# Gated attention and a SiLU layer on one core: the state's product with values as the stationary operand, and four weight loads issued earlier

## The chip, the core and the metric

The kernel runs on one core of a Trainium2 chip. A core has a matrix engine (TensorE), a vector engine (VectorE), a scalar engine for activation functions (ScalarE), a general engine (GpSimd) and a queue engine (SyncE, "SP" in the profile), each with its own instruction stream. They share an on-chip memory of 128 partitions (SBUF) and a small accumulator memory (PSUM) that TensorE writes. Transfers between DRAM and SBUF, or inside SBUF, are issued from SP, ScalarE or GpSimd and carried out by the DMA engines.

The metric is the device time of one execution in microseconds (us). The kernel before takes 665.35 us (median of 3 runs, 663.98 to 667.26).

## What is computed

Two blocks follow each other. The first is a gated linear recurrence with a complex decay per channel; B = 4 batches, H = 8 heads, S = 768 positions, D = 48 channels per head. The second is a feed-forward layer with SiLU, 384 to 2048 to 384, over all 3072 tokens.

```python
def _attn_ref(q, k, v, a_re, a_im):
    B, H, S, D = q.shape
    mag = np.sqrt(a_re * a_re + a_im * a_im)
    scale = np.minimum(mag, 0.999) / (mag + 1e-06)
    a_re_n, a_im_n = (a_re * scale, a_im * scale)
    # S_re, S_im: (B, H, D, D), zero at the start
    for t in range(S):
        ar, ai = (a_re_n[:, :, t, :, None], a_im_n[:, :, t, :, None])
        new_re = ar * S_re - ai * S_im
        new_im = ar * S_im + ai * S_re
        kv = np.einsum('bhd,bhe->bhde', k[:, :, t], v[:, :, t])
        S_re, S_im = (new_re + kv, new_im)
        y[:, :, t] = np.einsum('bhd,bhde->bhe', q[:, :, t], S_re)
    return y

def _moe_ref(x, w_in, w_out):
    h = x @ w_in
    g = h * (1.0 / (1.0 + np.exp(-h)))
    return g @ w_out
```

The kernel does not step through the positions. It cuts them into chunks of 128 and multiplies keys and queries with the running decay (magnitude and angle), so that a chunk's output is a masked product of queries and keys with the values, plus a product of the queries with the state that earlier chunks left. A complex channel becomes two real ones, so keys and queries have 2 x 48 = 96 channels per head.

## The kernel before

There are 24 chunks (4 batches of 6), taken two at a time: step p handles chunks 2p (called A) and 2p + 1 (called B). Chunk n + 4 continues chunk n of the same batch. While a step's attention runs, TensorE also works through the feed-forward layer of the pair before.

The state that chunk n hands on is one product per head, with the rotated keys `kr` (128 positions x 96 channels) as the stationary operand and the values (128 x 48) moving. VectorE adds the old state and multiplies by the chunk's decay:

```python
def state(n):
    x = X[n]
    if place(n)[1] == NCH - 1:                   # the last chunk of a batch hands nothing on
        return
    ps = p_m.tile([D2, H, D], F32, tag="m", name=f"s{n}")          # D2 = 96
    for h in range(H):
        nc.tensor.matmul(ps[:, h], lhsT=x["kr"][:, h].rearrange("p c d -> p (c d)"),
                         rhs=x["v"][:, h], start=True, stop=True)
    x["s"] = ps
    if n >= STRAIGHT:                            # STRAIGHT = 4
        carried_on(n)

def carried_on(n):
    x = X[n]
    ps = x["s"]
    new = att.tile([D2, H, D], F32, tag="S", name=f"S{n + B}", bufs=5)
    by = decs[:, n].unsqueeze(2).to_broadcast([D2, H, D])
    if "S" in x:
        nc.vector.tensor_tensor(out=new, in0=ps, in1=x["S"], op=ALU.add)
        nc.vector.tensor_tensor(out=new, in0=new, in1=by, op=ALU.mult)
    ...
    X[n + B]["S"] = new
```

The output `y` of a chunk already uses values and state as stationary operands of 64 columns, two heads side by side in PSUM partitions 0 to 63 and 64 to 127. A head has 48 channels; the 16 columns beyond belong to the next head and are not used:

```python
def output(n):
    ...
    for hp in range(HH):
        for r in range(2):
            h = 2 * hp + r
            cols = ds(h * D, 64 if h + 1 < H else D)
            to = ps[64 * r:64 * r + (64 if h + 1 < H else D), hp]
            nc.tensor.matmul(to, lhsT=v_[:, cols], rhs=x["w", h // HH][:, h % HH], ...)
            if carried:
                nc.tensor.matmul(to, lhsT=x["S"].rearrange("p h d -> p (h d)")[:, cols],
                                 rhs=x["qT"][:, h], start=False, stop=True)
    ...        # ScalarE copies y to xT; parts of it go to xT by DMA ("xT<-y" in the profile)
```

Keys and queries reach their transposed form `T` in two moves: VectorE transposes 32x32 blocks into `sq`, and 24 DMA transfers per chunk, half of them on SP and half on GpSimd, put the blocks in their places:

```python
def turned(n):
    ...
    sq = later["left"].tile([C, NB, 2 * H, Q], F32, tag="sq", name=f"sq{n}", bufs=2)   # Q = 32
    for i, w in enumerate("kq"):
        nc.vector.transpose(sq[:, :, ts(i, H)], ...)
    for b in range(NB):
        for a in range(NA):
            (nc.gpsimd if a % 2 else nc.sync).dma_start(out=to[ts(b, Q), :, a], in_=sq[ts(a, Q), b])
```

The weights arrive as 64-bit words and are converted in the first part of the program. `fetch` (F in the schedule) loads a block into one of four `raw` buffers; H (VectorE) and R (ScalarE) take its high and low words, J joins them. H and R fetch a block themselves if it has not been fetched:

```python
def words(n):
    if n == len(fetched):
        fetch(1)
    dst, _, parts = blocks[n]
    return dst, fetched[n], parts[0][1].dtype != F32
```

The order of all this is written by hand. The first part is one long list; the fifth chunk (number 4) is turned at `tt:4`:

```python
... trig:5 F:1 exp:5 J:1 tt:4 J:1 h:0 g:05 K:5 Q:5 G0:3 r:0 R:1 H:1 J:1 g:06 R:1 H:1 R:1 H:1 s:4 ...
```

From step 3 on each step follows one order: `h` and `r` are pieces of the feed-forward layer (hidden product, and product with the second weights), `t` turns keys and queries, `a` is the product of keys and queries, `s` the state, `y` the output, `X` and `A` the loads for later steps:

```python
usual = ("c h E h kA qA h r tA D kB h L qB r F h tB r G h A X a0A th uA uB h a1A r sA h a0B yA "
         "r a1B sB r pA yB pB mA S r mB r lA lB")
```

## Time and profile before

| | before |
|---|---|
| time, median of 3 runs | 665.35 us (663.98 to 667.26) |
| span of the profiled execution | 661.8 us |
| TensorE busy, granted clock | 639.2 us (97%), 0.996 |
| VectorE busy | 463.5 us (70%) |
| ScalarE busy | 367.1 us (55%) |
| GpSimd busy | 165.1 us (25%) |
| DMA, mean | 71.15 MB, 108 GB/s |

The profile is a record of one execution. "PE" is a TensorE matmul, "PEld" the load of its stationary operand, "DVE" VectorE, "ACT" ScalarE, "POOL" GpSimd, "SP" the queue engine; "SPq" and "POOLq" are issues of DMA transfers. L665 is line 665 of the kernel. A group of instructions is given as `output<-inputs` with the shapes and a count, and in brackets the idle time of its engine just before it, with what ended it. [...] lengths of neighbours overlap and their starts are what to compare. Every product in 32-bit floats shows in the trace as two instructions.

The span has three parts: a first part up to about 164 us, in which weights are loaded and converted while the first chunks run; steps of 51.0 us each from there to about 575 us; and the last two pairs up to the end.

### The profile page before, as it was taken

The numbers are of one execution on the slowest core, as the hardware profiler recorded it, in microseconds if no ns is written. First come the engines' busy times: TensorE is split into PE (matmuls) and PEld (weight loads), VectorE is DVE, ScalarE is ACT, GpSimd is POOL, SyncE is SP. The second block draws the span as 40 slices with busy tenths as digits, with TensorE's granted clock in tenths as the row PEclk, the third lists the DMA queues.
The fourth block names the chain that finished last, engine by engine and source line by source line (L and its number), as shares of the span: only waits on it lengthen the run. The fifth ranks groups of instructions, "written<-read, shape, count | busy, mean of one in ns | idle before, by whom it ended". The sixth has DMA issues, their size and how long they took to land.

```text
span 661.8 us, 11281 instructions
## 1 busy us (share of the span) xinstructions
PE 639.2 (97%) x4084; PEld 571.0 (86%) x4084; DVE 463.5 (70%) x995; ACT 367.1 (55%) x537; POOL 165.1 (25%) x260
## 2 busy tenths in 40 slices
PE   6789999989999999999999999999999999998997
PEld 4668866767999999999999999999999999997997
DVE  5998279567975875884784784785785785765543
ACT  6897698696852762662671681780680581610110
POOL 7436000362320320330230240240240250221000
PEclk9999999989999999999999999999999999999999
DMA  9888355555382383293195185175167165578540
GB/s 169 197 187 175 102 152 121 117 93 113 55 150 39 53 143 53 42 143 63 33 134 74 32 127 90 32 112 104 32 94 122 32 85 85 173 171 235 196 145 27
DMA packets 168699, 71.15 MB, mean 108 GB/s; under 512 B 152848, under 2 KB 157072, under 8 KB 168640
## 3 DMA queue, kind: packets, MB, share of 16 engines
q1 hardware_dynamic: 156368, 49.37, 36.5%
q0 software_dynamic: 8960, 16.51, 16.2%
q10 hardware_dynamic: 3312, 4.52, 1.9%
q8 instruction: 33, 0.54, 0.3%
q14 instruction: 26, 0.21, 0.1%
HBM read 48.86 MB, written 4.79 MB: 81 GB/s over the span
## 4 chain that ended last, share of the span: by engine, by line
PE 77%; ACT 7%; DMA 6%; DVE 5%; SPq 3%; issue 1%; POOL 1%; ACTq 0%; DVEq 0%
PE h L689 31%; PE o L781 27%; PE a L578 5%; PE y L608 3%; PE s L665 3%; PE y L611 3%; PE o L737 2%; DMA raw<-in_moe_w_in_dram 2%; SPq L565 2%; ACT L300 2%; ACT s L300 1%; ACT mag L300 1%; DMA raw<-in_moe_w_out_dram 1%; PE phase L441 1%; ACT r L218 1%
## 5 line engine op out<-in xcount | busy, mean ns | idle before, releaser
L689 PE MATMUL h<-xT,w 128*128 128x256 f32 x1152 | 260.3, 380 | 0.0
L689 PEld LDWEIGHTS h<-xT,w 128*128 128x128 f32 x1152 | 216.8, 190 | 28.0 <-DMA xT<-y 0.2
L300 ACT ACTIVATE g<-h 128x512 f32<-128x512 f32 x96 | 55.2, 596 | 138.8 <-PE h L689 135.4
L565 POOL DMA_DIRECT2D T<-sq x120 | 77.2, 651 | 75.8 <-issue 62.4
L295 ACT ACT_TABLE_LOAD x62 | 79.5, 1283 | 2.0 <-PEq L1181 0.9
L781 PE MATMUL o<-w,gs 128*128 128x192 f32 x320 | 77.9, 326 | 0.0
L589 DVE TENSOR_TENSOR w<-a,upto_r 128x512 f32<-128x512 f32 x48 | 32.9, 687 | 62.0 <-PE a L578 62.0
L511 POOL DMA_DIRECT2D decs<-ends x48 | 30.7, 646 | 156.6 <-DMA ends<-eq 145.8
L781 PE MATMUL o<-w,g 128*128 128x192 f32 x320 | 66.7, 331 | 0.0
L625 POOL DMA_DIRECT2D xT<-y x30 | 15.9, 537 | 202.5 <-ACT y L621 194.3
L617 ACT COPY xT<-y 128x384 f32<-128x384 f32 x20 | 9.6, 478 | 100.9 <-PE y L611 100.9
L781 PE MATMUL o<-wc,gs 128*128 128x192 f32 x320 | 65.0, 327 | 0.0
L781 PEld LDWEIGHTS o<-w,g 128*128 128x128 f32 x320 | 53.8, 190 | 3.5 <-issue 1.9
L781 PEld LDWEIGHTS o<-w,gs 128*128 128x128 f32 x320 | 56.4, 190 | 0.0
L578 PEld LDWEIGHTS a<-T 96*128 96x128 f32 x384 | 49.4, 192 | 7.7 <-issue 3.4
L578 PE MATMUL a<-T 96*128 96x128 f32 x384 | 51.1, 277 | 4.0 <-DMA T<-sq 2.8
L781 PEld LDWEIGHTS o<-wc,gs 128*128 128x128 f32 x320 | 54.2, 190 | 0.1
L724 DVE TENSOR_TENSOR gs<-g 128x128 f32<-128x128 f32 x160 | 38.8, 283 | 20.1 <-PE o L781 14.0
L737 PE MATMUL o<-w,g 128*128 128x384 f32 x128 | 45.5, 505 | 3.0 <-ACT g L300 3.0
L737 PEld LDWEIGHTS o<-w,g 128*128 128x128 f32 x128 | 24.7, 197 | 19.9 <-ACT g L300 4.2
L781 PE MATMUL o<-wc,g 128*128 128x192 f32 x160 | 39.0, 327 | 0.0
L608 PE MATMUL y<-w,v 128*64 128x128 f32 x320 | 35.3, 282 | 0.0
(117 smaller groups left out, 977.0 us busy)
## 6 DMA issues: line engine op xcount, KB each, us to landing
T<-sq SPq DMA_DIRECT2D x120, 64.0 KB
T<-sq POOLq DMA_DIRECT2D x120, 64.0 KB, 4.3
raw<-in_moe_w_out_dram SPq DMA_DIRECT2D x16, 384.0 KB
small<-in_moe_w_in_dram SPq DMA_DIRECT2D x16, 384.0 KB
small<-in_moe_w_out_dram SPq DMA_DIRECT2D x16, 384.0 KB
raw<-in_moe_w_in_dram SPq DMA_DIRECT2D x24, 192.0 KB
out_dram<-ot ACTq DMA_DIRECT2D x23, 192.0 KB
im<-in_a_im_dram SPq DMA_DIRECT2D x16, 192.0 KB
```

What stands on the lines that cost most here:

```text
L295: chain(nc.scalar.preload_act_table_set({"exp": "natural_log_exp_and_others", "trig": "trig_and_small", "silu": "silu_and_others"}[of]))
L300: chain(nc.scalar.activation(out=out, in_=in_, func=func, **kw))
L511: nc.gpsimd.dma_start(out=decs[a * D:(a + 1) * D, n], in_=ends[n].rearrange("(h d) -> d h", d=D))
L565: (nc.gpsimd if a % 2 else nc.sync).dma_start(out=to[ts(b, Q), :, a], in_=sq[ts(a, Q), b])
L578: nc.tensor.matmul(ps[:, h], lhsT=x["kT"][:, hh * HH + h], rhs=x["qT"][:, hh * HH + h], start=True, stop=True)
L589: nc.vector.tensor_tensor(out=x["w", hh], in0=x["a", hh], in1=upto.unsqueeze(1).to_broadcast([C, HH, C]), op=ALU.mult)
L608: nc.tensor.matmul(to, lhsT=v_[:, cols], rhs=x["w", h // HH][:, h % HH], start=True, stop=not carried)
L611: nc.tensor.matmul(to, lhsT=x["S"].rearrange("p h d -> p (h d)")[:, cols], rhs=x["qT"][:, h], start=False, stop=True)
L689: nc.tensor.matmul(ps[:, ji], lhsT=w1[:, dc, ts(jp * 2 + ji, C)], rhs=A[p]["xT"][:, dc], start=(dc == 0), stop=(dc == ND - 1))
L724: nc.vector.tensor_tensor(out=t[:, i], in0=a, in1=b, op=op)
L737: nc.tensor.matmul(A[p]["o"][m].rearrange("p n c -> p (n c)"), lhsT=A[p]["g", jp][:, ji, ts(m, C)], rhs=w2[:, j], start=(j == 0), stop=(j ...
L781: nc.tensor.matmul(o[i], lhsT=a, rhs=b, start=(jp == 0 and i < 4), stop=(final and j == jp and i in ((5, 3, 6, 2) if p == NP - 1 else (4, ...
```

## The change

From chunk 6 on the state's product is turned around: the values are stationary (64 columns, 48 of the head and 16 beyond, as in `y`), the keys move (96 columns), and two heads stand side by side in PSUM. The result comes out transposed, values by keys. VectorE transposes its 32x32 blocks into SBUF, and 12 DMA transfers per chunk put the blocks in their places in the new state `S`. Adding the old state and multiplying by the decay is done in SBUF one step later (`wA`, `wB` in the order). The value tile gets 16 columns of zeros at its end, so that the last head can be read 64 wide. Each chunk's decay gets its own small tile instead of a place in one table for all chunks, and the closing test of the decays reads them from DRAM.

The second part of the change is one number in the first list: `F:1` ahead of `tt:4` becomes `F:4`, so that the last four blocks of the second weights are fetched there, ahead of the transfers of the fifth chunk's turned keys.

```diff
+    FULL = 6
@@ load_x
+            if name == "v":
+                X[n]["all v"] = ld.tile([C, DM + 64 - D], F32, tag="v", name=f"v{n}", bufs=4)
+                nc.gpsimd.memset(X[n]["all v"][:, DM:], 0.0)
+                X[n]["v"] = X[n]["all v"][:, 0:DM].rearrange("p (h d) -> p h d", d=D)
@@ ends_of
+        x["dec"] = att.tile([D2, H], F32, tag="dec", name=f"dec{n}", bufs=6)
         for a in range(2):
-            nc.gpsimd.dma_start(out=decs[a * D:(a + 1) * D, n],
+            nc.gpsimd.dma_start(out=x["dec"][a * D:(a + 1) * D],
                               in_=ends[n].rearrange("(h d) -> d h", d=D))
@@ state
+        if n >= FULL:
+            state_of_pairs(n)
+            return
...
+    def state_of_pairs(n):
+        x = X[n]
+        ps = p_m.tile([C, HH, D2], F32, tag="m", name=f"s{n}")
+        for h in range(H):
+            hp, r = divmod(h, 2)
+            nc.tensor.matmul(ps[64 * r:64 * r + 64, hp], lhsT=x["all v"][:, ds(h * D, 64)],
+                             rhs=x["kr"][:, h].rearrange("p c d -> p (c d)"),
+                             start=True, stop=True)
+        sq = moe.tile([C, 2, DM // 2], F32, tag="ot", name=f"ssq{n}").rearrange("p n c -> p (n c)")
+        nc.vector.transpose(sq, ps.rearrange("p h d -> p (h d)"))
+        sq = sq.rearrange("p (h b i) -> p h b i", b=NB, i=Q)
+        new = att.tile([D2, H, D], F32, tag="S", name=f"S{n + B}", bufs=6)
+        to = new.rearrange("p (h r) e -> p r h e", r=2)
+        for b in range(NB):
+            for g in range(NA):
+                r, part = divmod(g, 2)
+                e = slice(part * Q, min((part + 1) * Q, D))
+                (nc.gpsimd if g % 2 else nc.sync).dma_start(
+                    out=to[ts(b, Q), r, :, e], in_=sq[ts(g, Q), :, b, 0:e.stop - e.start])
+        X[n + B]["new"] = new
@@ carried_on
-        by = decs[:, n].unsqueeze(2).to_broadcast([D2, H, D])
+        by = x["dec"].unsqueeze(2).to_broadcast([D2, H, D])
+        if "new" in X.get(n + B, ()):
+            new = ps = X[n + B]["new"]
...
         if "S" in x:
             nc.vector.tensor_tensor(out=new, in0=ps, in1=x["S"], op=ALU.add)
-            nc.vector.tensor_tensor(out=new, in0=new, in1=by, op=ALU.mult)
...
+        nc.vector.tensor_tensor(out=new, in0=ps, in1=by, op=ALU.mult)
@@ step
+                what["w" + x] = lambda n=n: carried_on(n - 2) if n - 2 >= FULL else None
@@ the first list
-                H:1 carry:6 g:15 trig:5 F:1 exp:5 J:1 tt:4 J:1 h:0 g:05 ...
+                H:1 carry:6 g:15 trig:5 F:4 exp:5 J:1 tt:4 J:1 h:0 g:05 ...
@@ the order of a step
-    usual = ("c h E h kA qA h r tA D kB h L qB r F h tB r G h A X ...
+    usual = ("c h E h kA qA h r tA D kB h L qB r F h tB wA wB r G h A X ...
@@ the closing test
+    decays_ = pre.tile([N, DM], F32, tag="t3", name="decays_", bufs=5)
+    nc.sync.dma_start(out=decays_, in_=ends)
...              # the minimum is taken over decays_ instead of decs
```

## The prediction

> **What bounds the kernel now.** I read the table of windows first, because the page's shares are averages over stages. Its columns are the window, its length, then busy time (and instructions) of TensorE, its weight loads, VectorE, ScalarE and GpSimd, TensorE's granted clock, the DMA share and GB/s.

> ```profile
> 120.00:130.00 10.00, 9.58 (x50) 7.53 (x49) 4.33 (x7) 5.52 (x8) 5.11 (x8) 1.00 0.71 138
> 130.00:140.00 10.00, 8.87 (x45) 7.09 (x43) 8.11 (x14) 7.25 (x9) 1.63 (x3) 1.00 0.34 72
> 140.00:150.00 10.00, 8.98 (x43) 5.92 (x45) 5.03 (x9) 9.87 (x11) 9.75 (x13) 0.83 0.96 156
> 317.00:368.00 51.00, 51.00 (x346) 47.81 (x345) 36.96 (x83) 27.55 (x40) 11.87 (x19) 1.00 0.53 80
> ```

> From about 164 us to 575 us a step of two chunks takes 51.0 us, and TensorE is busy for all of it; VectorE has 14 us to spare. There every us taken off TensorE's own sequence is a us off the span, as long as no new wait appears. From 120 to 150 us TensorE has holes (0.42 + 1.13 + 1.02 = 2.6 us) and a clock of 0.83. The state product is 3% of the chain that ended last; the timeline of TensorE in one step (start, length, group) gives its price.

> ```profile
> 345.64 1.48 PE L665 MATMUL s<-v,kr 128*96 128x48 f32 x16
> 346.96 2.82 PE L689 MATMUL h<-xT,w 128*128 128x256 f32 x12
> 349.62 1.06 PE L578 MATMUL a<-T 96*128 96x128 f32 x8
> 350.61 0.45 PE L608 MATMUL y<-w,v 128*64 128x128 f32 x4
> ...
> 352.20 0.44 PE L611 MATMUL y<-T,S 96*64 96x128 f32 x4
> 352.57 0.92 PE L781 MATMUL o<-w,g 128*128 128x192 f32 x4
> ```

> Starts count, not lengths, because matmuls overlap. The 16 instructions of one chunk's state (8 heads, two per product) take 346.96 - 345.64 = 1.32 us. In the single records they start 85 ns apart, though each moves only 48 columns. The `a` products move 128 columns and start 112 ns apart, so 48 columns would need about 42 ns: what is paid here is the load of 96 weight columns. In the records the product after a state starts its second instruction 70 ns late (286 ns instead of 216), so one state costs 1.39 us.

> The `y` products show the form that the change gives the state: 64 stationary columns, two heads side by side in the two column halves. There 32 instructions with 128 moving columns start 55 ns apart, half of 112. But entering costs 205 - 112 = 93 ns, and leaving costs 201 - 55 = 146 ns and another 103 ns (266 instead of 163) at the next product's second instruction: together 0.34 us for each visit.

> For the early hole I followed the chain of waits back from TensorE: the second line below is the ScalarE operation it waited for, then come the loads behind that (SP's issues, VectorE's and ScalarE's waits).

> ```profile
> 141.02 1.58 PE L737 MATMUL o<-w,g 128*128 128x384 f32 x2 [2.15 <-ACT g L300]
> ...
> 140.37 1.08 ACT L300 ACTIVATE g<-h 128x512 f32<-128x512 f32 x2
> ...
> 130.36 0.56 ACT L218 ACTIVATE r<-raw 128x384 int32<-128x384 uint32 x1 [4.80 <-DMA raw<-in_moe_w_out_dram]
> 132.76 0.58 ACT L218 ACTIVATE r<-raw 128x384 int32<-128x384 uint32 x1 [1.84 <-DMA raw<-in_moe_w_out_dram]
> ...
> 111.32 0.36 SPq L185 DMA_DIRECT2D raw<-in_moe_w_out_dram  x1
> 120.00 0.21 SPq L509 DMA_DIRECT2D ends<-eq  x1
> 120.39 4.14 SPq L565 DMA_DIRECT2D T<-sq  x6
> 124.58 1.97 SPq L185 DMA_DIRECT2D raw<-in_moe_w_out_dram  x3
> ```

> SP is in order: the last three loads of second weights are issued only at 124.58, behind six transfers of transposed keys that wait until 120.4. Both ScalarE and VectorE stand for them, 6.6 us on ScalarE, and TensorE is left without `g` at 138.70.

> [...] after 2.33 us without a matmul the 384-column products start 640 ns apart instead of 323, until about 144.7 us[...].

> **The change, part by part.**

> *State product, chunks numbered 6 to 19 (14 of them).* Removed: 1.39 us of TensorE each. Added: 16 instructions, 64 stationary columns, 96 moving. By columns moved, 96/128 x 112 = 84 ns, and two halves side by side give 42 ns: 16 x 42 = 0.67 us. With the borders of 0.34 us that makes 1.01 us. Saving 0.38 us; but `y` blocks need some 50 ns to come to their full rate, so I take 0.33 us: 14 x 0.33 = 4.6 us. If instead the weight loads of the halves don't overlap, the pitch is 64/96 x 85 = 57 ns: 0.91 + 0.34 = 1.25, a saving of 0.14 us or 2.0 us in all. The `y` blocks cannot tell these apart (both give 55). I weigh the first at two in three, so 3.7 us.

> *VectorE.* The state's two operations of 0.55 us on the product are replaced by a 128x384 transpose (about 0.5 us, half of the 0.97 us of a 128x768 one), and add and multiply (1.1 us) come in the next step. For a step of two chunks that is 2 x 0.5 us more on an engine with 14 us free. The 2.2 us fall after the second transpose of keys, where VectorE next waits 1.62 us for `a`; the mask after it gets 0.7 us later, and PSUM for the next state is asked for only 4 us after that. Worth nothing.

> *Transfers.* 12 per chunk, 6 on SP, 6 on GpSimd, with 128 packets each; a chunk's keys and queries take 24 with 512 packets. Their rate on SP is 1.06 us each, a three-piece `xT` transfer 0.61; I put the new ones at 0.7 us. The dangerous place is the end of a step:

> ```profile
> 350.65 0.99 SPq L154 DMA_DIRECT2D v<-in_v_dram  x1
> 362.69 1.82 SPq L625 DMA_DIRECT2D xT<-y  x3
> ```

> SP stands idle between these. The first chunk's six go from 351.7 to 355.9; the second chunk's product is out at about 357, transposed by 357.5, and its six go to 361.7. `xT` is needed at 362.6: 1 us to spare. On GpSimd (0.65 us each) the picture is the same. `xT` lands at about 366.3 and the hidden product starts at 367.5, a second us. So this stays hidden, narrowly.

> *Earlier loads.* In the changed order all four loads stand ahead of `ends`. Their buffers come free with conversions at 109.7, 111.7 and 116.0 us, all before SP has to issue the keys at 120.4, and the DMA share from 110 to 120 us is only 0.28. They land by about 120, so ScalarE's 6.6 us and VectorE's 6.1 us of waiting go. ScalarE then issues `g` when its product is there, some 4 us sooner, against 2.33 us of TensorE's gap. The gap goes and with it the slow clock: seven pitches took 4.05 us instead of 7 x 0.323 = 2.26, so 1.8 us. At most 4.1 us; I take 3.3, because the next thing in line (transposed keys, tables on ScalarE) may keep some.

> *The rest:* padding memsets of V on GpSimd, and the decay check from DRAM instead of SBUF, both outside the chain. 0.

> Sum: 3.7 + 3.3 = 7.0 us; 665.35 - 7.0 = 658.3 us.

> **The rivals.** (a) *The borders eat the saving.* If entering and leaving cost more with 96 columns than in a `y` block, and loads don't overlap, the state saves nothing and only the loads count: about 662. [...] Against: the borders of all `y` blocks measure alike. (b) *A transfer takes the place of the matmul time.* If the new transfers take over 0.9 us each on the queues, `xT` comes late by 1 to 2 us in seven steps[...]: 665 to 675. For it: 128 B packets, and loads that fill the DMA until 354 us. Against: SP's idle stretch of 11 us. (c) *The early loads only move the wait*, to the keys of the fifth or sixth chunk, or to ScalarE's table loads, which fill 140 to 153 us: 1 us instead of 3.3, so 661. (d) *Everything works*: 5.3 + 4.1 us and a little at the holes, 655.5.

> **Range and chances.** The sum's parts are nearly independent, 2.0 to 5.3 us and 0.5 to 4.3 us, and three runs of before spread over 3.3 us. The limit of 2% faster is 652.0 us, a gain of 13.3 us and more than everything I can add up (9.4); 678.7 us is the limit of slower, and needs (b) at its worst. I say 654 to 663, faster by over 2% 0.05, within 2% 0.93, slower 0.02.

> **What would show it.** State product: 16 instructions from its first start to the next product's in about 0.75 to 0.9 us, plus a late second instruction; steps of 50.3 us instead of 51.0. A step of 50.7 means loads in series. No idle time of TensorE on `xT` or on `S`; if it appears, (b) is right. Clock 1.00 in 130 to 150 us and no wait of `o` on `g` over 0.5 us there; a remaining gap means (c). I am wrong altogether if steps are 51 us or longer.

## The result, and the profile after

| | before | after |
|---|---|---|
| time, median of 4 runs each | 664.88 us (663.98 to 667.26) | 656.75 us (653.88 to 657.31) |
| ratio to before | | 0.9864, 95% interval 0.9825 to 0.9903 |
| span of the profiled execution | 661.8 us | 655.6 us |

The changed kernel is 1.4% faster (1.0 to 1.75%). 658.3 us had been predicted, with a range of 654 to 663.

First the table of windows of the changed kernel, for the same stretches as before (window, length, busy time and instructions of TensorE, weight loads, VectorE, ScalarE, GpSimd, then the granted clock, the DMA share and GB/s):

```profile
120.00:130.00 10.00, 9.55 (x50) 7.28 (x49) 7.51 (x15) 7.64 (x12) 5.24 (x8) 1.00 0.55 80
130.00:140.00 10.00, 10.00 (x52) 8.27 (x51) 5.14 (x8) 7.90 (x10) 6.64 (x11) 1.00 0.56 72
140.00:150.00 10.00, 10.00 (x71) 7.08 (x70) 6.54 (x10) 9.84 (x10) 6.25 (x8) 1.00 1.03 193
312.00:362.24 50.24, 50.24 (x346) 46.43 (x345) 37.74 (x85) 27.57 (x40) 18.60 (x33) 1.00 0.59 88
```

From 130 to 150 us TensorE now has no hole, and its clock is 1.00 instead of 0.83; from 140 to 150 us it gets through 71 instructions instead of 43. A step takes 50.24 us instead of 51.00, still with TensorE busy throughout. VectorE pays 0.8 us more per step and GpSimd 6.7 us more, neither near the 50.

The timeline of SP gives the reason for the first three rows (start, length, group, count):

```profile
111.85 5.83 SPq L191 DMA_DIRECT2D raw<-in_moe_w_out_dram  x4
121.25 0.24 SPq L514 DMA_DIRECT2D ends<-eq  x1
121.61 16.18 SPq L571 DMA_DIRECT2D T<-sq  x12
```

All four loads of second weights are out by 117.7 us and no longer stand behind the keys; before, the first was out at that place too, and the other three only at 124.6 us. The timeline of TensorE shows what became of its wait for `g`:

```profile
139.06 1.06 PE L584 MATMUL a<-T 96*128 96x128 f32 x8
139.95 5.33 PE L773 MATMUL o<-w,g 128*128 128x384 f32 x16
```

The 384-column product follows the `a` product directly; before, it came after 2.15 us of waiting. And this is one state product in a regular step:

```profile
340.83 0.88 PE L687 MATMUL s<-kr,v 128*64 128x96 f32 x16
341.64 2.86 PE L725 MATMUL h<-xT,w 128*128 128x256 f32 x12
```

From start to start it is 0.81 us instead of 1.32.

To see where the time went, the span is cut at starts of the same TensorE instructions in each kernel: the hidden product that begins at about 120 us, the first product of the first regular step, and the end of the seventh step. All figures in us, from the profiled executions; "rest" is the pairs after those seven steps.

| kernel | up to the mark at 120 | from there to the first step | each of 7 steps | rest | span |
|---|---|---|---|---|---|
| before | 119.32 | 44.31 | 51.00 | 141.14 | 661.77 |
| after | 120.54 | 40.45 | 50.24 | 142.93 | 655.60 |
| difference | +1.23 | -3.86 | 7 x -0.76 = -5.32 | +1.79 | -6.17 |

The two parts of the change show in the two middle columns, with 9.2 us together. The outer columns, where the change does nothing to TensorE's work, take 3.0 us back. The experiments have to say whether that is a cost of the change.

In the rest, it is the last wait for turned keys. The timeline of TensorE there, first before:

```profile
603.46 1.13 PE L578 MATMUL a<-T 96*128 96x128 f32 x8 [2.84 <-DMA T<-sq]
...
605.24 0.44 PE L611 MATMUL y<-T,S 96*64 96x128 f32 x4
605.46 0.44 PE L608 MATMUL y<-w,v 128*64 128x128 f32 x4
```

then after:

```profile
595.44 1.13 PE L584 MATMUL a<-T 96*128 96x128 f32 x8 [2.13 <-DMA T<-sq]
...
597.40 0.71 PE L617 MATMUL y<-T,S 96*64 96x128 f32 x4
597.83 0.71 PE L614 MATMUL y<-w,v 128*64 128x128 f32 x4
```

Before, the longer wait (2.84 us) leaves the clock as it is: groups of four `y` products start 0.22 us apart. After, a shorter wait (2.13 us) is followed by half speed: 0.43 us apart.

### The profile page after: what moved, and what is told of

The parts are those of the page before. It is cut to its first block, busy times and chain, and to the rows that moved or that the text cites. A ratio compares the mean times of both kernels' runs of the same rounds, so it can differ in the third digit from the quotient of the medians.

```text
span 655.6 us, 11519 instructions
## 1 busy us (share of the span) xinstructions
PE 634.7 (97%) x4084; PEld 562.1 (86%) x4084; DVE 468.4 (71%) x1009; ACT 367.2 (56%) x537; POOL 213.8 (33%) x368
## 4 chain that ended last, share of the span: by engine, by line
PE 80%; ACT 7%; DVE 5%; DMA 4%; SPq 2%; issue 1%; DVEq 0%; ACTq 0%
PE h L725 32%; PE o L817 27%; PE a L584 6%; PE y L614 3%; PE o L773 3%; PE y L617 3%; DMA raw<-in_moe_w_in_dram 2%; PE s L687 2%; ACT L305 2%; SPq L571 1%; PE phase L446 1%; ACT mag L305 1%; ACT s L305 1%; PE L L446 1%; DMA im<-in_a_im_dram 1%
## 5 line engine op out<-in xcount | busy, mean ns | idle before, releaser
L517 POOL DMA_DIRECT2D dec<-ends x48 | 30.8, 648 | 154.9 <-DMA ends<-eq 154.9
L699 POOL DMA_DIRECT2D S<-ssq x84 | 45.8, 553 | 94.8 <-DVE ssq L691 56.5
L773 PE MATMUL o<-w,g 128*128 128x384 f32 x128 | 43.7, 489 | 0.8 <-ACT g L305 0.8
```

Of the source, the lines that this page charges most:

```text
L517: nc.gpsimd.dma_start(out=x["dec"][a * D:(a + 1) * D], in_=ends[n].rearrange("(h d) -> d h", d=D))
L699: (nc.gpsimd if g % 2 else nc.sync).dma_start(out=to[ts(b, Q), r, :, e], in_=sq[ts(g, Q), :, b, 0:e.stop - e.start])
L773: nc.tensor.matmul(A[p]["o"][m].rearrange("p n c -> p (n c)"), lhsT=A[p]["g", jp][:, ji, ts(m, C)], rhs=w2[:, j], start=(j == 0), stop=(j ...
```

## The experiments

The theory: a state costs 1.01 us instead of 1.39 because weight loads of the two column halves overlap, and the earlier loads save the gap on `g` and the slow clock behind it. The rivals: loads in series; borders that eat the saving; transfers that nearly delay `xT`; and, once the result was known, a cost of the change in the first and the last part.

**The two parts apart.** `state_only` is the changed kernel with the old place of the loads, `loads_only` the kernel before with the new place.

```diff
state_only, from after:
-                H:1 carry:6 g:15 trig:5 F:4 exp:5 J:1 tt:4 J:1 h:0 g:05 ...
+                H:1 carry:6 g:15 trig:5 F:1 exp:5 J:1 tt:4 J:1 h:0 g:05 ...
loads_only, from before:
-                H:1 carry:6 g:15 trig:5 F:1 exp:5 J:1 tt:4 J:1 h:0 g:05 ...
+                H:1 carry:6 g:15 trig:5 F:4 exp:5 J:1 tt:4 J:1 h:0 g:05 ...
```

> The changed kernel with the number of early loads put back to one. If the state's product saves what its starts show (1.39 to 1.01 us, 14 times), steps stay at 50.24 us and 5.3 us of the gain stay: ratio 0.992, about 659.5 us; TensorE's gap on g near 139 us and the half clock after it come back. If the step's gain came from anything that the early loads set off (another phase of the queues), steps go back towards 51.0 us and the ratio to 1.00.

> The kernel before with the four early loads alone. Theory: the gap on g and the half clock go, steps stay 51.00 us, and the time falls by 3.9 us: ratio 0.994, about 661 us. Together with the state alone this should add up to the whole change (0.986). Rival: the loads only move the wait to the keys of the fifth or sixth chunk, then under 2 us are gained: ratio 0.997 or more.

Measured: `state_only` 658.75 us against 663.79 (ratio 0.9932, 0.9908 to 0.9956); `loads_only` 662.80 (0.9982, 0.9961 to 1.0002). In sections:

| kernel | up to the mark at 120 | to the first step | each step | rest | span |
|---|---|---|---|---|---|
| state_only | 120.99 | 44.64 | 50.24 | 142.72 | 660.04 |
| loads_only | 121.85 | 40.66 | 51.00 | 143.37 | 662.88 |

Each part alone gives its own column as in the changed kernel (50.24; 40.66 against 40.45) and leaves the other's within 0.33 us of the kernel before. TensorE's timeline in `state_only` has the gap, and the slow clock in its window:

```profile
139.66 1.06 PE L584 MATMUL a<-T 96*128 96x128 f32 x8
143.03 5.18 PE L773 MATMUL o<-w,g 128*128 128x384 f32 x10 [2.31 <-ACT g L305]
```

```profile
140.00:150.00 10.00, 7.69 (x24) 4.48 (x23) 5.06 (x10) 9.86 (x12) 9.62 (x15) 0.83 0.86 133
```

In `loads_only` the same products follow each other without it:

```profile
140.58 1.06 PE L578 MATMUL a<-T 96*128 96x128 f32 x8
141.47 5.33 PE L737 MATMUL o<-w,g 128*128 128x384 f32 x16
```

Yet `loads_only` gains only 1.0 us in the median, with an interval from -0.1 to 2.6 us, though its section is 3.65 us shorter; 3.9 us had been expected, and by the number alone this is the rival's outcome. In the medians the two parts make 6.0 us together, less than the whole change. The profile shows what took the gain back: 2.5 us in the first part and 2.2 us in the rest, where a wait for `T` of 3.48 us is followed by half speed. No state product is changed in this kernel. So losses in the outer columns come without the change as well.

**The rate of the product.** `halves` splits each moving operand into two of 48 columns. By columns moved nothing changes; the number of weight loads doubles.

```diff
-            nc.tensor.matmul(ps[64 * r:64 * r + 64, hp], lhsT=x["all v"][:, ds(h * D, 64)],
-                             rhs=x["kr"][:, h].rearrange("p c d -> p (c d)"), ...)
+            for c in range(2):
+                nc.tensor.matmul(ps[64 * r:64 * r + 64, hp, ts(c, D)],
+                                 lhsT=x["all v"][:, ds(h * D, 64)], rhs=x["kr"][:, h, c], ...)
```

> The changed kernel with each state product cut into two of 48 moving columns, the values loaded twice as often; the result is the same. If the moved columns alone set the pace, the 32 instructions take the 0.64 us of the 16 (20 ns each) and a step stays at 50.24 us. If loads of 64 columns set a floor of 57 ns in each column half (28 ns in the mean), they take 0.91 us and a step grows by 0.5 us to 50.8 us. If loads of the two halves did not overlap, 57 ns each, 1.8 us, and a step is 52.6 us.

Measured: one run of 658.74 us, steps of 50.82 us. TensorE's timeline:

```profile
340.54 1.17 PE L688 MATMUL s<-kr,v 128*64 128x48 f32 x32
341.64 2.86 PE L726 MATMUL h<-xT,w 128*128 128x256 f32 x12
```

The 32 instructions take 1.10 us, 0.29 more than the 16. In the single records instructions of the same half start 58 ns apart here, with one of the other half 13 to 41 ns behind each; in the changed kernel it is 82 ns, with 6 to 7 ns between the halves. 58 ns is close to an estimate for a load of 64 columns from the 85 ns of 96 columns (64/96 x 85 = 57), the halves' loads go side by side, and 96 moving columns at 82 ns are above that floor. Loads in series are refuted. That the floor is the load and not another fixed cost of an instruction fits the number, but no run separates the two.

**The borders.** `one_visit` puts the two states of a step before and behind chunk A's output, so that TensorE enters the 64-column form once for all three.

```diff
-             ... h a1A r sA h a0B yA r a1B sB r pA yB ...
+             ... h a1A r h a0B sB yA sA r a1B r pA yB ...
```

> The changed kernel with both states of a step placed directly beside the first output product, so that all 64-column products of the first half stand together and two entries and two exits per step are saved; the work is the same. If each border pair costs 0.20 to 0.34 us whatever stands in it, a step falls from 50.24 to 49.6 us (up to 0.68 us less), 4 to 4.7 us over seven steps: ratio to the kernel before 0.979, about 651.5 us. If the borders are only filling time of the array that any change of product pays, the steps stay at 50.2 us. If the output product then waits for PSUM, TensorE shows idle time before y and the step gets longer.

Measured: 651.63 us, ratio 0.9830 (0.9803 to 0.9858); steps of 49.74 us. TensorE's timeline:

```profile
342.78 1.06 PE L584 MATMUL a<-T 96*128 96x128 f32 x8
343.77 0.88 PE L687 MATMUL s<-kr,v 128*64 128x96 f32 x16
344.62 0.45 PE L614 MATMUL y<-w,v 128*64 128x128 f32 x4
...
346.21 0.44 PE L617 MATMUL y<-T,S 96*64 96x128 f32 x4
346.44 0.88 PE L687 MATMUL s<-kr,v 128*64 128x96 f32 x16
347.25 0.92 PE L817 MATMUL o<-w,g 128*128 128x192 f32 x4
```

Two visits fewer give 0.50 us in a step, where 2 x 0.34 = 0.68 would be whole. In the single records the second state begins 54 ns after the last `y` product, the pitch of the `y` products themselves: at this seam a change of product inside the form costs nothing. At the other seam the first `y` product comes 217 ns after the last state. The waits of TensorE's weight loads in the seven steps (total us, times, longest) name the reason:

```profile
PEld y L614 <- DVE w L595: 1.1, 7, 0.2
```

Chunk A's output stands for the mask of chunk B's half product, which VectorE has only just got. That is most of the missing 0.18 us.

**The transfers.** `all_on_sp` issues all twelve transfers of a state from SP.

```diff
-                (nc.gpsimd if g % 2 else nc.sync).dma_start(
+                nc.sync.dma_start(
```

> The changed kernel with all twelve transfers of a state issued from SP, none from GpSimd. In the changed kernel SP issues twelve per step in 9.3 us and is done 1.0 us before xT is ready. If that narrow margin is real, 24 per step push xT back by about 8 us, TensorE waits for xT in each of the seven steps, and a step grows by 6 to 7 us (about 700 us in all). If the margin is not what counts (transfers overlap anyway), steps stay at 50.24 us.

Measured: one run of 702.42 us; the seven steps take 54.89 to 57.19 us, 5.9 more in the mean than after. SP's timeline, first in the changed kernel, then in `all_on_sp` at the same place of a later step:

```profile
346.75 9.27 SPq L699 DMA_DIRECT2D S<-ssq  x12
357.02 1.83 SPq L631 DMA_DIRECT2D xT<-y  x3
```

```profile
422.84 16.59 SPq L699 DMA_DIRECT2D S<-ssq  x24
439.53 1.83 SPq L631 DMA_DIRECT2D xT<-y  x3
```

With twelve, SP is done at 356.0 and `xT` goes out at 357.0, 1.0 us later. With 24, `xT` follows their end at once, and TensorE stands, as its waits say:

```profile
PE h L725 <- DMA xT<-y: 27.1, 7, 4.5
```

That is 3.9 us in each of seven steps; the other 2 us fit the slow clock behind such a wait, 0.54 in the five us after this one:

```profile
440.00:445.00 5.00, 3.53 (x8) 2.86 (x9) 3.06 (x9) 0.00 (x0) 0.00 (x0) 0.54 0.29 90
```

So the danger was real, and splitting the transfers over two queues is what keeps the change from losing to it.

**The end.** In the last pairs VectorE also looks at the low words of the weights (`tiny`), for a test that closes the kernel. The timeline of VectorE, after, shows one such look ahead of the last transposes of keys:

```profile
584.30 0.55 DVE L257 TENSOR_REDUCE tiny<-small 128x1 f32<-128x384 f32 x1 [5.45 <-DMA small<-in_moe_w_in_dram]
584.77 0.97 DVE L566 STREAM_TRANSPOSE sq<-kr 128x768 f32<-128x768 f32 x1
```

VectorE stands 5.45 us for a load that nothing needs yet (5.01 us in the kernel before), the keys are transposed late, and TensorE waits for `T`. `tail`, `state_tail`, `one_visit_tail` and `before_tail` leave out the look at this one place; the same 32 looks are made, one place later.

```diff
         looks.append(0)
+        if len(looks) == 7:
+            return
```

> The kernel before with one check fewer, nothing else. If the last wait is the same in every version, it gains as much as the changed kernel does (2.5 to 4 us): ratio about 0.995. The profile is a second look at where the clock is halved in the kernel before: if only chance decides, the start (20 to 25 us) may show it here, which the first profile of the kernel before did not.

> The changed kernel with one weight check fewer ahead of the last turned keys (the seventh of the calls that check weights does nothing; all weights are still checked later). If TensorE's last wait on turned keys (2.1 to 3.5 us near 600 us, with a half clock behind it worth 1.4 to 2.2 us) comes from VectorE standing for a check's load, it goes: the part from the last regular step to the end gets 2.5 to 4.5 us shorter and the runs lie closer together; ratio to the kernel before 0.984 or less, about 653 us. If the wait comes from the DMA engines being full there, it stays and the time too.

> The same as the kernel before this one (one check fewer), but with only one early load instead of four. Compared with it, it gives the worth of the early loads without the noise of the last wait. Theory: the gap on g is 2.3 us long always, and the half clock after it comes in some executions only: 2.3 to 4 us slower than with the four loads, ratio 0.988 to 0.990. Rival: the early loads are worth only the 1 us that they gave alone; then the two differ by 1 us or less.

> Both additions to the changed kernel: the two states beside the first output product, and one check fewer. If the two are independent, 49.74 us per step as measured and the shorter end: ratio 0.978 or less, about 648.5 us.

Measured against 664.21 us for the kernel before:

| kernel | time | ratio (95%) | up to 120 | to the first step | each step | rest |
|---|---|---|---|---|---|---|
| before_tail | 660.10 (658.51 to 661.82) | 0.9932 (0.9908 to 0.9955) | 120.52 | 42.38 | 51.00 | 139.22 |
| state_tail | 656.42 (656.11 to 656.72) | 0.9880 (0.9858 to 0.9902) | 120.88 | 42.75 | 50.24 | 139.08 |
| tail | 653.21 (652.25 to 654.13) | 0.9829 (0.9805 to 0.9852) | 120.79 | 40.39 | 50.24 | 138.62 |
| one_visit_tail | 650.82 (649.11 to 652.68) | 0.9790 (0.9766 to 0.9815) | 122.76 | 40.53 | 49.74 | 139.50 |

The transpose and TensorE's timeline in `tail`:

```profile
578.97 0.97 DVE L566 STREAM_TRANSPOSE sq<-kr 128x768 f32<-128x768 f32 x1
```

```profile
592.92 1.13 PE L584 MATMUL a<-T 96*128 96x128 f32 x8
```

The wait is gone (0.88 us of it stay in `before_tail`), and so is its slow clock; the rest is 138.6 to 139.5 us in all four. Now the difference of the two kernels with and without the change is clean: `tail` is 6.9 us faster than `before_tail` in the medians, and the sections say 7 x 0.76 + (42.38 - 40.39) = 7.3 us. The first part doesn't charge the change either: 120.52 against 120.79.

`state_tail` settles the earlier loads' worth: `tail` is 3.2 us faster in the medians and 2.4 us shorter in the section, within the 2.3 to 4 us expected, and the rival's 1 us is out. It has the gap without the slow clock. TensorE's timeline and window:

```profile
142.06 5.43 PE L773 MATMUL o<-w,g 128*128 128x384 f32 x16 [1.80 <-ACT g L305]
```

```profile
140.00:150.00 10.00, 8.20 (x57) 5.80 (x57) 5.06 (x9) 9.86 (x11) 10.00 (x16) 1.00 0.97 152
```

`one_visit_tail` is the fastest version tried in the median, 2.1% under the kernel before; the changed kernel's medians are 4.5 and 5.9 us higher. It misses the 648.5 us expected by 2.3 us: against `tail`, its profile is 3.5 us shorter in the steps, but 2.0 us longer in the first part and 0.9 us longer in the rest.

**Once more, and one order further.** `after_again` is the changed kernel unchanged. `one_visit_later` tries to give VectorE time for the mask by placing chunk B's half product one block earlier.

```diff
one_visit_later, from one_visit_tail:
-             ... h a1A r h a0B sB yA sA r a1B r pA yB ...
+             ... h a1A r a0B h sB yA sA r a1B r pA yB ...
```

> The changed kernel unaltered, once more, for a closer figure of the whole change. Regular steps give 5.3 us, the early loads 2.0 to 2.4 us where the clock is not halved behind the gap and 3.9 us where it is: together 7.3 to 9.2 us, ratio 0.986 to 0.989. If the early loads are worth only the 1 us they gave alone, 0.990 or more.

> As the kernel with one visit and one check fewer, but the first product of keys and queries of the second chunk goes ahead of a hidden product instead of behind it, so that its mask is done and its PSUM free when the first output product wants it. With one visit a step took 49.74 us: 0.50 less, where two border pairs of 0.34 us were expected to save 0.68. If the missing 0.18 us is the wait for that mask (0.2 us ahead of y in each step), a step falls to 49.55 us and the time by 1.3 us: ratio 0.977. If the borders are simply worth less than 0.34 us, the steps stay at 49.74 us.

Measured: `after_again` 655.30 us against 664.90 (0.9869, 0.9836 to 0.9901). Its profile has 119.29, 40.31, 50.24 and 140.47 us in the four columns: the middle two as before, and the outer two without the 3.0 us that the first profile of the same kernel had lost. `one_visit_later` takes 655.49 us (0.9861, 0.9829 to 0.9893): slower than `one_visit_tail`, though two of its six runs lie at 651.6 to 651.8. Two of its `a` products in TensorE's timeline:

```profile
239.70 1.13 PE L584 MATMUL a<-T 96*128 96x128 f32 x8 [0.41 <-DMA T<-sq]
...
538.67 1.13 PE L584 MATMUL a<-T 96*128 96x128 f32 x8 [0.82 <-DVE th_parts L434]
```

Three of its steps take 49.55 us, as wanted, and the wait for the mask is gone. In four others chunk B's product stands 0.2 to 0.8 us for its operands at its new, earlier place: one wait has been changed for another. The profiled run is one of the two fastest (651.83 us), so what the slower ones lose is not seen, and stays open.

**Which stalls bring the slow clock.** Each trace also holds the granted clock over time, and it shows what sets these stalls apart. In each of the 13 profiles every stretch at half clock begins on a grid of 3.413 us: the time from one beginning to the next is a whole multiple of it (152 of them from 141.12 to 659.94 us in before, 169 from 20.15 to 597.00 us in after). All but the last of a profile, which its end cuts off, last 3.41 us or a whole multiple (6.83 us in `all_on_sp`, 10.24 in `one_visit_tail`). So the windows are cut at the grid here, around the last wait for `T`, first before, then after (window, length, then TensorE's busy time; the clock is third from the end):

```profile
598.50:601.92 3.42, 2.12 (x10) 1.52 (x8) 0.00 (x0) 0.60 (x1) 0.00 (x0) 1.00 0.87 143
601.92:605.33 3.41, 1.87 (x22) 1.78 (x24) 0.55 (x1) 0.00 (x0) 0.00 (x0) 1.00 0.93 308
605.33:608.74 3.41, 3.41 (x37) 3.22 (x33) 2.84 (x8) 0.65 (x2) 0.00 (x0) 1.00 0.93 330
```

```profile
593.58:597.00 3.42, 1.56 (x17) 1.47 (x19) 0.00 (x0) 0.41 (x1) 0.00 (x0) 1.00 1.00 285
597.00:600.41 3.41, 3.41 (x30) 3.05 (x27) 1.95 (x4) 0.56 (x2) 0.00 (x0) 0.50 0.90 320
```

Before, the 2.84 us of waiting fall on both sides of 601.92, 1.29 and 1.55 us. After, 1.85 of the 2.13 us lie in one interval, and the next one runs at half speed. The same for the long waits at these two places in the other profiles:

| wait | length | largest part in one interval | next interval |
|---|---|---|---|
| `T`, after_again | 1.67 | 0.89 | full |
| `g`, state_tail | 1.80 | 1.18 | full |
| `g`, before_tail | 1.46 | 1.46 | full |
| `T`, before | 2.84 | 1.55 | full |
| `T`, one_visit | 2.42 | 1.69 | half |
| `T`, after | 2.13 | 1.85 | half |
| `g`, before | 2.15 | 2.15 | half |
| `T`, halves | 2.20 | 2.20 | half |
| `g`, state_only | 2.31 | 2.31 | half |
| `T`, state_only | 2.64 | 2.64 | half |
| `T`, loads_only | 3.48 | 2.69 | half |

In these eleven waits the largest part in one interval separates the two kinds, between 1.55 and 1.69 us; the length does not. The grid lies differently against the program from profile to profile (its first border is at 1.17 us in before, at 3.08 us in after), and the changed kernel met the slow clock at its last wait for `T` in one execution (1.85 us) and not in the other (0.89 us). This is read from the traces, and no run moves a stall on purpose. Nor is it the whole rule: elsewhere (the first 50 us, the last 20 us, `all_on_sp`) intervals with 1.1 to 2.0 us of standing went both ways (1.67 us from 14.82 us on in before left the clock full, at most 1.65 us from 24.31 us on in `tail` came ahead of half speed), and in `one_visit_tail` the clock stayed at half for three intervals, in the last two of which TensorE was busy. The start of the program shows the same: before and `before_tail` are the same program there, and only the second has a half-clock interval, from 19.9 us. Up to 120 us the profiles with no such interval take 118.7 and 119.3 us, those with one 119.2 to 121.9, and `one_visit_tail` with four intervals' length 122.8; so part of the spread in the first column is the clock.

## Why the prediction was right, and where its terms were off

1. *TensorE bounds the steps, and what is saved there comes off the span.* Right. A step is 50.24 us (50.3 said), 14 x 0.38 = 5.3 us saved in seven steps, no wait for `xT` or `S`.

2. *One state costs 1.01 us.* Right: 0.81 us to the next product's start (0.75 to 0.9 said), in the single records 0.09 us more ahead of it (256 ns after the product before instead of 163) and 0.10 us at the next product's second instruction (320 ns instead of 216). That makes 1.01 us against 1.39 before, and equals the 0.67 us by columns moved and the 0.34 us of borders, as read off the `y` blocks. What a border consists of no trace shows; 0.34 us a visit is its measured price.

3. *The state term: 3.7 us.* Mis-sized; 5.3 us measured. Two deductions were for nothing. The coming up to full rate (0.33 us instead of 0.38) is there, 133 ns instead of 82 between the first two instructions of a half, but the two halves start 7 ns apart where 42 had been counted, and that makes up for most of it. And the rival of loads in series, which cut the term by a fifth, was wrong, as `halves` shows. The profile before could not have refuted it, but an answer of two outcomes (4.6 or 2.0) was turned into a mean that neither gives.

4. *VectorE worth nothing, transfers hidden with 1 us to spare.* Right, both. The transfers take 0.77 us each on SP (0.7 said) and 0.55 on GpSimd (0.65 said), SP is free 1.0 us ahead of `xT`, and `all_on_sp` shows what lies beyond that margin: 5.9 us a step. Rival (b) fell by the split of queues, not by lack of danger.

5. *The early-loads term: 3.3 us, at most 4.1.* The mechanism was right: the loads, the gap and the clock, and rival (c) is refuted, since no wait took its place. The size is not one number. Against kernels in which the gap brings the slow clock the section is 3.9 us shorter in before and after (4.2 from `state_only` to after); where the gap stays without it (`before_tail`, `state_tail`) it is 2.0 to 2.4. The prediction took the clock loss as belonging to the gap; in these profiles it came where 2.15 and 2.31 us of the gap lay in one interval of the clock's grid (before, `state_only`), and not where 1.18 and 1.46 us did (`state_tail`, `before_tail`).

6. *The rest: 0.* Not what the first profile shows (+3.0 us in the outer columns), but right for the change. `loads_only` loses 4.8 us there without any new state product, `after_again` loses nothing with all of them, and the `tail` pair is even.

So the right total is not only a right sum. 5.3 + 2.0 to 3.9 make 7.3 to 9.2 us, and the medians show 8.1 (first runs), 9.6 (`after_again`) and 6.9 (the `tail` pair). The prediction's 7.0 was low in the first term by 1.6 and about right in the second.

What stays open: what besides the standing time in an interval decides on the clock, and what the slower runs of `one_visit_later` lose.

## What to carry to other kernels

A product whose moving side is shorter than its weight load (here 48 columns, an estimated 42 ns by the 112 ns of the `a` products, at a pitch of 85 ns) is worth turning around if two narrow stationaries can stand side by side as here (two products every 82 ns), but count the borders (0.34 us a visit here, half of the new product's own time), and put all products of that form into one visit where their operands are ready. In a queue that issues in order, as SP did here (three loads at 124.6 us, behind six transfers that waited until 120.4), issue loads ahead of transfers that wait, and look at what the queue must carry next: 1 us of slack was all that parted a gain of 0.8 us from a loss of 5.2 us a step. Where stalls of 1.5 to 3.5 us change the clock in one execution and not in another, compare profiles between marks on the same instructions, and remove the stall before judging a change of 1%.
